# A GpSimd word read ahead of weight loads, weight-quarter sums on VectorE alone, and a re-planned order of 1,784 operations, in a chunk-selecting attention followed by a gated feed-forward layer

## The chip, the cores and the metric

The kernel runs on one core of one Trainium2 chip. The core's engines are named here as the profile names them: PE (TensorE matmuls) with PEld (its weight loads), DVE (VectorE), ACT (ScalarE), POOL (GpSimd) and SP (SyncE, which here only issues DMAs). The metric is device microseconds of one execution; the median over several executions is compared.

## The reference: what is computed

Attention over 4 batches, 8 heads, 768 positions, 64 dimensions, in which each query may only look at 6 of the 24 chunks of 32 keys, and then a gated layer over all 3072 tokens:

```python
ub = np.sum(np.maximum(q[:, :, :, None, :] * k_min[:, :, None, :, :], q[:, :, :, None, :] * k_max[:, :, None, :, :]), axis=-1)
ub = np.where(causal, ub, -1000000000.0)
top_chunks = np.argsort(ub, axis=-1)[..., -top_k:]
scores = scale * np.matmul(q, k.transpose(0, 1, 3, 2))      # only selected chunks, causal
attn = softmax(scores); attn_out = np.matmul(attn, v)
gate = 1.0 / (1.0 + np.exp(-(x @ w_gate)))                  # x: [3072, 512], w_gate: [512, 1536]
val = x @ w_val
return (gate * val @ w_out).astype(np.float32)              # w_out: [1536, 512]
```

## The kernel before, in words

**Units.** The 24 blocks of 128 queries are worked in eight units of three blocks, u0 to u7. Unit u0 (and one block of u2) holds "first" blocks, whose queries see fewer than six chunks, so that nothing is selected: function `first` turns keys and queries on PE (`kfT`, `qfT`), copies them to fp16 (`kf16`, `qf16`), makes scores (`scf`), exponentials on ACT (`expf`), zeroes the upper triangle on POOL (`cmf`), multiplies with the values (`pvf`), divides (`rzf`, `xf` on DVE), turns the result (`xpsf`) and copies it into the unit's input of the feed-forward layer (`xTf`). The other units also compute bounds for each chunk (`ub`), transpose them (`ubn`), take the eight largest (`mx`, a chain of MAX8), mark the rest (`ap`, `apt`) and add the marks to the queries (`hqm`), and then go through `attend` (scores `sc`, `exp`, triangle `cm`, values `pv`, division `rz` and `x`, turn `xps`, copy `xT`).

**Feed-forward.** For each unit, function `ffn` (lines 883 to 912) makes, for each of 12 column blocks, four matmuls `g` with the gate weights and four `v` with the value weights (line 898), a tanh on ACT (line 906) and one product on DVE (`hg`, line 910); `project_out` (lines 914 to 942) multiplies with the output weights (`o`, line 929), copies to SBUF (`osb`) and stores (`out`). Units u5 and u6 are worked together by `ffn_pair` (lines 963 to 1067) in a scheme with seven products for eight: it needs sums of quarters of the gate and value weights, four for each (`Sg0` to `Sg3`, `Sv0` to `Sv3`, function `mixed`, line 958, each 128x1536 fp16), and sums of halves of the units' inputs (`T0` to `T3`, line 980).

**Loads.** Attention inputs are loaded from SP's queue: `kf`, `qf`, `vf` for the first blocks of batches 0 to 2 (for k and q in two pieces each, 128 KB; v 256 KB), then `kq_u` for unit 1 (eight loads of 192 KB), value blocks `v`, `kq_u` for unit 2 and so on. The weights (three column parts `wg0..2`, `wv0..2` and three row parts `wo0..2`, each read as fp32 and cast to fp16, 512 KB) are loaded from POOL's queue (lines 470 to 476). A DMA issue stands in its engine's stream like any other instruction; what is behind it waits for it.

**What sets the order.** No scheduler decides at build time. A string `ORDER` (lines 94 to 258) names every operation once, in the order in which it is emitted, with `@ENGINE` where another than the first listed engine takes it and `:n` for the buffer slots. Each engine executes its own operations in that order. The dependencies that a `plan.add` lists (its `reads`, `writes` and `deps`) were for the planner that wrote the string; in the built program an instruction waits only for what it really touches: the data it reads and the buffers it overwrites. A load of weights touches nothing that an attention load writes, so in the program the weight loads wait for nothing but their place in POOL's stream, although their `plan.add` lists a load of queries (line 1087) or the operation `cmf_2_1` (line 1088) ahead of them. SP's loads reuse eight completion semaphores in turn, so each waits for the landing of the load eight places before it.

**POOL's stream at the start** of the program before: constants, the mask pattern (`epat`, line 439), two copies into the key tiles (`hkf1`, `hkp111`), `wg0`, `wv0`, the two `cmf_0`, the two `cmf_1`, `v16_0_0`, `vc_2` (the cast of the third first block's values, which waits for the load `vf_2`), the two `cmf_2`, `wg1`, `wv1`, `wg2`, `wv2`, one key copy, `wo0`, `wo1`, `wo2`.

Of the kernel before, what the change touches and what calls it, by code (L numbers as in the profile page):

```python
# [94 lines left out]
vf1_3:0 kf0_0:0 v10 ap0 vf1_2:1 ident hq1 kf1_0 epat0:0 vf1_1:2 qf0_0:1 ident16 v11 hq0 epat kcr0 qf1_0 ap1 kcr1  # L95
qf0_1:2 kf1_1:3 kfT_0:0 qf1_1 hkp001 kf0_1 hkp000 hkp101@ACT kf0_2:4 qfT_0:1 kf16_0@DVE:3 vf_1:5 hkp011 hkf0@ACT
qf16_0@DVE:4 hkf1 hkp100 hkp110@ACT scf_0:2,3,1 qf1_2:0 kxf1:0 qf0_2 expf_0_0 kxf0 hkp111@POOL kf1_2 qfT_1:4
expf_0_1:2 kcr_f vf_0:1 hkp010 kfT_1:5 qf16_1:5 wg0 wv0 kf16_1:6 vf_2:3 vc_1@ACT scf_1:6,7,3 cmf_0_0 expf_1_1:0
cmf_0_1 k1_u1:0 qfT_2:1 expf_1_0 cmf_1_1 k2_u1 kfT_2:2 cmf_1_0 qf16_2:3 pvf_1_1:0 pvf_1_0:3 kf16_2:4 rzf_1_1:0 k0_u1
v16_0_0 xf_1_1:0 scf_2:4,5,3 rzf_1_0:1 k3_u1 xf_1_0:1 xpsf_1_1:7,0 pvf_0_0:6 q2_u1 expf_2_0 xTf_1_1 pvf_0_1:1  # L100
xpsf_1_0:2 vc_2 rzf_0_0:0 q3_u1 expf_2_1:1 rzf_0_1:1 xf_0_0:2 cmf_2_0 q0_u1 xf_0_1:0 kn_u1_1:5 xpsf_0_0:0 xTf_1_0
q1_u1 xTf_0_0@ACT xpsf_0_1:3 cmf_2_1 pvf_2_0:7 kT_u1_1:4 xTf_0_1 rzf_2_0:0 wg1 xf_2_0:1 pvf_2_1:6 kt_u1_1:0 rzf_2_1:1
xpsf_2_0:5 xf_2_1:2 wv1 hk0_u1_1@ACT v_0_1:5 xTf_2_0 xpsf_2_1:1 kx1_u1_1:1 kn_u1_2:6 wg2 xTf_2_1 kn_u1_0:2 kT_u1_2:2
kx0_u1_1 wv2 hk1_u1_1@ACT g_u0_0:0,0,0 kt_u1_2:1 v_0_2:0 kn_u1_3@DVE:3 kx0_u1_2 hk1_u1_2@ACT hk0_u1_2@POOL v_u0_0:3
wo0 kx1_u1_2 tanh_u0_0 wo1 g_u0_1:7,1,1 hg_u0_0 wo2 kT_u1_0:6 tanh_u0_1 v_u0_1:5 kt_u1_0:2 g_u0_2:1,2,2 hk0_u1_0
hk1_u1_0@ACT hg_u0_1 v_u0_2:4 tanh_u0_2 kx0_u1_0 g_u0_3:2,3,3 kx1_u1_0 hg_u0_2 kT_u1_3:0 tanh_u0_3 v_u0_3:3
qn_u1_2@DVE:4 kt_u1_3:0 g_u0_4:7,0,4 hk1_u1_3 hk0_u1_3@ACT kx1_u1_3 qT_u1_2:5 tanh_u0_4 hg_u0_3 qf_u1_2:0 kx0_u1_3
v_0_3:4 qn_u1_3@POOL:5 qm_u1_2@ACT:0 hq0_u1_2@DVE hq1_u1_2 qT_u1_3:1 qn_u1_0@DVE:1 v_u0_4:6 k1_u2:1 kcr_u1 qf_u1_3
qn_u1_1@DVE:6 qT_u1_0:4 hq0_u1_3@DVE hq1_u1_3 g_u0_5:2,1,5 hg_u0_4 qf_u1_0 qm_u1_3@POOL qT_u1_1:7 tanh_u0_5 qm_u1_0
v_u0_5:3 hq0_u1_0@DVE hq1_u1_0 qf_u1_1@DVE g_u0_6:5,2,6 hg_u0_5 qm_u1_1@ACT hq0_u1_1@POOL v_u0_6:0 tanh_u0_6  # L110
hq1_u1_1@DVE ub_u1:1,6 hg_u0_6 g_u0_7:4,3,7 ubn1_u1:0 k2_u2 v16_0_1 ubn0_u1 v_u0_7:2 tanh_u0_7 k0_u2 ubm1_u1 ubm0_u1
mx1_u1:0 g_u0_8:7,0,8 mx0_u1 v_u0_8:3 tanh_u0_8 g_u0_9:5,1,9 ap1_u1 ap0_u1 hg_u0_8 v_u0_9:0 tanh_u0_9 apt0_u1:0
g_u0_10:6,2,10 apt1_u1 hg_u0_9 hqm0_u1_0@ACT hqm0_u1_2 v_u0_10:1 tanh_u0_10 hqm1_u1_0@DVE sc_u1_0_2:4,0 hqm1_u1_2@DVE
sc_u1_1_2:7,2 sc_u1_4_2:3,3 exp_u1_0_2 g_u0_11:5,0,11 hg_u0_10 exp_u1_1_2 hg_u0_7 exp_u1_4_2 sc_u1_3_2:0,1 sc_u1_3_1:6
tanh_u0_11 v_u0_11:4 exp_u1_3_2 exp_u1_3_1 k3_u2 sc_u1_0_0:1 v16_0_2 hg_u0_11 sc_u1_3_0:7 q0_u2 exp_u1_0_0 o0_u0_0:3,0
q1_u2 exp_u1_3_0 cm_u1_0 sc_u1_4_1:2 sc_u1_1_0:5 cm_u1_3 exp_u1_4_1 sc_u1_4_0:0 o1_u0_0 exp_u1_1_0 exp_u1_4_0 cm_u1_1
sc_u1_1_1:6 sc_u1_0_1:4 exp_u1_1_1 cm_u1_4 o2_u0_0 exp_u1_0_1 q2_u2 v16_0_3 o0_u0_1:1,1 v_0_4:1 osb_u0_0 kn_u2_1@DVE:2
pv_u1_3:7 out_u0_0 kn_u2_2@DVE:3 kT_u2_1:2 sc_u1_2_0:5,1 kn_u2_0@DVE:4 sc_u1_2_2:0 kt_u2_1:1 kT_u2_2:6 q3_u2
exp_u1_2_0 kT_u2_0:4 kn_u2_3@DVE:5 sc_u1_2_1:3 kx0_u2_1 hk1_u2_1@POOL o1_u0_1 v_0_5:3 exp_u1_2_2 kx0_u2_2
qn_u2_0@POOL:1 exp_u1_2_1 kx1_u2_2:0 qn_u2_1@POOL:6 kt_u2_0:2 pv_u1_1:5 kx1_u2_1 cm_u1_2 kf0_3:2 kt_u2_2:0 pv_u1_0  # L120
kx0_u2_0 hk1_u2_0@ACT kT_u2_3:0 qn_u2_2@POOL:2 kx1_u2_0 qT_u2_1:3 pv_u1_2 kx1_u2_3 hk0_u2_2@ACT hk1_u2_2@POOL kf1_3
sc_u1_5_2:2,2 qf_u2_1:1 v16_0_4 sc_u1_6_2:6,0 rz_u1_0:0 sc_u1_5_1:4 kx0_u2_3 exp_u1_5_2 o2_u0_1 qf0_3:5 kt_u2_3@DVE:0
exp_u1_5_1 hq1_u2_1@POOL x_u1_0:0 exp_u1_6_2 kcr_u2@POOL qf1_3 hk0_u2_3@POOL qT_u2_2:3 qn_u2_3:3 rz_u1_1:1
sc_u1_7_2:2,1 qm_u2_1:0 xps_u1_0:0,1 hq0_u2_1 vf_3:0 sc_u1_5_0:4 x_u1_1:1 hk0_u2_0@POOL qT_u2_3:6 xT_u1_0@ACT
sc_u1_7_0:5 qf_u2_2@DVE hk0_u2_1@POOL exp_u1_7_2 pv_u1_4:7 qf_u2_3@DVE hk1_u2_3@POOL exp_u1_5_0 xps_u1_1:0 k00_1:0
sc_u1_6_0:3 v16_0_5 osb_u0_1@DVE qT_u2_0:2 hq0_u2_3 o0_u0_2:6,0 cm_u1_5 xT_u1_1 qf_u2_0 exp_u1_7_0 qm_u2_3 qm_u2_0
pv_u1_5 qm_u2_2 hq0_u2_0 sc_u1_7_1:4 hq1_u2_3@DVE sc_u1_6_1:1 ub_u2:0,2 exp_u1_6_0 rz_u1_2:0 cm_u1_7 x_u1_2:2
exp_u1_7_1 hq0_u2_2@POOL exp_u1_6_1 hq1_u2_2@DVE pv_u1_7:5 hq1_u2_0@DVE xps_u1_2:3 out_u0_1 vc_3@ACT ubn1_u2:0 cm_u1_6
qfT_3:7 k01_1 xT_u1_2 kfT_3:4 mx1_u2:0 qf16_3:4 pv_u1_6 o1_u0_2 kf16_3:5 ubn0_u2 rz_u1_3:1 ap1_u2 x_u1_3:0 scf_3:1,2,3
o2_u0_2 apt1_u2:0 expf_3_1:2 k10_1 mx0_u2 hqm1_u2_0 expf_3_0 xps_u1_3:3 osb_u0_2 xT_u1_3 cmf_3_1 sc_u2_5_1:7,1  # L130
sc_u2_4_0:0,0 exp_u2_5_1 g_u1_0:4,1,12 ap0_u2 hqm1_u2_2@DVE exp_u2_4_0 apt0_u2 cmf_3_0 v_u1_0:5 tanh_u1_0
hqm0_u2_0@DVE g_u1_1:2,2,13 hqm0_u2_2@DVE hg_u1_0 cm_u2_4 out_u0_2 v_u1_1:1 tanh_u1_1 k11_1 sc_u2_5_2:3 pvf_3_0:6
hg_u1_1 g_u1_2:7,3,14 exp_u2_5_2 rzf_3_0:0 xf_3_0:1 v_u1_2:0 tanh_u1_2 sc_u2_0_0:4,3 hg_u1_2 sc_u2_0_1:5 q01_1:1
exp_u2_0_0 sc_u2_0_2:2 xpsf_3_0:1,0 pvf_3_1:3 g_u1_3:6,0,15 exp_u2_0_2 xTf_3_0 cm_u2_0 rzf_3_1:1 exp_u2_0_1 xf_3_1:2
v_u1_3:7 tanh_u1_3 sc_u2_1_2:0,2 sc_u2_1_0:4 hg_u1_3 exp_u2_1_2 g_u1_4:1,1,16 exp_u2_1_0 sc_u2_1_1:2 tanh_u1_4
pv_u2_0:3 cm_u2_1 xpsf_3_1:5 exp_u2_1_1 q00_1 sc_u2_4_1:6 kx0_1_1 k16_1_2:6 sc_u2_6_2:7,3 v_u1_4:0 exp_u2_4_1 kx0_1_2
k16_1_1:2 exp_u2_6_2 sc_u2_6_0:4 g_u1_5:1,2,17 xTf_3_1@ACT exp_u2_6_0 kx1_1_1:1 k16_1_3:3 v_u1_5:2 k16_1_0@ACT:1
cm_u2_6 pv_u2_1 kx1_1_2 tanh_u1_5 sc_u2_6_1:6 sc_u2_4_2:7 sc_u2_2_1:5,2 exp_u2_6_1 g_u1_6:4,3,0 kt_1_1:4 exp_u2_4_2
sc_u2_2_2:1 exp_u2_2_1 v_u1_6:6 kx0_1_0 q11_1 hk0_1_1 exp_u2_2_2 pv_u2_4:7 tanh_u1_6 sc_u2_2_0:5 kt_1_0:5 hk1_1_1
sc_u2_3_1:1,0 exp_u2_2_0 g_u1_7:4,0,1 kx1_1_0 exp_u2_3_1 hk1_1_0 sc_u2_3_2:5 tanh_u1_7 sc_u2_3_0:1 kt_1_2:0  # L140
hk0_1_0@ACT cm_u2_2 q10_1 v_u1_7:4 exp_u2_3_0 hg_u1_6 exp_u2_3_2 hk1_1_2@DVE g_u1_8:6,3,2 rz_u2_0:0 cm_u2_3 hg_u1_4
hk0_1_2@ACT sc_u2_5_0:1 x_u2_0:0 v_u1_8:5 tanh_u1_8 hg_u1_5 v_1_1:4 exp_u2_5_0 pv_u2_2:0 kt_1_3:2 xps_u2_0:3 pv_u2_3
cm_u2_5 xT_u2_0@ACT g_u1_9:6,1,3 kx0_1_3 hk1_1_3@ACT hk0_1_3 pv_u2_5 sc_u2_7_2:2,2 rz_u2_1:1 kx1_1_3 tanh_u1_9
sc_u2_7_0:1 v_u1_9:3 exp_u2_7_2 v_1_3:1 exp_u2_7_0 qf0_u3_2:0 g_u1_10:6,2,4 kcr_1@POOL k01_2:0 qf0_u4_1:1 cm_u2_7
sc_u2_7_1:2 hg_u1_9 tanh_u1_10 v16_1_1 exp_u2_7_1 qf0_u3_1 v_u1_10:1 qf0_u3_3 g_u1_11:6,1,5 qf0_u3_0 qm_u3_2@ACT:0
hq0_u3_2@POOL k00_2 x_u2_1:1 tanh_u1_11 rz_u2_2:0 hg_u1_10 hq1_u3_0@POOL pv_u2_7:3 qm_u3_0@ACT xps_u2_1:2 qf0_u4_0
v_u1_11:0 xT_u2_1 v16_1_3 hq0_u3_0@ACT x_u2_2:2 ub_u3:6,1 hg_u1_11 hq1_u3_2@POOL hg_u1_8 hg_u1_7 xps_u2_2:2 pv_u2_6
xT_u2_2 o0_u1_0:7,1 ubn0_u3:0 rz_u2_3:1 ubn1_u3 o1_u1_0 ubm0_u3 qf0_u4_3 mx0_u3:0 o2_u1_0 ubm1_u3 x_u2_3:0 o0_u1_1:0,0
mx1_u3 osb_u1_0 k10_2 ap0_u3 o1_u1_1 ap1_u3 apt0_u3:0 apt1_u3 o2_u1_1 hqm0_u3_0@DVE hqm0_u3_2@ACT hqm1_u3_2@DVE
# [1043 lines left out]
```

## Time and profile before

| | us |
|---|---|
| median of 3 runs | 299.01 (298.44 to 300.31) |
| the profiled execution, whole | 297.33 |
| its span, first to last instruction | 295.6 |
| PE busy in the span | 274.8 |
| DVE busy | 221.1 |
| ACT busy | 203.9 |
| POOL busy | 99.1 |
| granted TensorE clock | 1.0 throughout |

The profile shows one execution. Rows of its timeline give start and duration in microseconds, the engine, the source line, and the tiles written and read; a bracket gives the idle time of that engine just before and what ended it. "Landing" of a DMA is the time from its issue until its data are there. PE's spans are modelled ends, and PE instructions overlap by some 0.1 to 0.2 us in them, so the busy time of a stretch, not the sum of single durations, says how full PE is. The same holds to a smaller degree for DVE and ACT.

### The profile page before, as it was taken

What the parts mean: (1) busy time and instruction counts of PE and PEld (TensorE: products, weight loads), DVE (VectorE), ACT (ScalarE), POOL (GpSimd) and SP (SyncE); (2) the same over time, 40 slices, a digit from 0 to 9 for tenths busy, and PEclk for the clock granted to TensorE, in tenths of its full rate; (3) what the DMA queues carried; (4) which work ended last, traced back from release to release, by engine and by line L of the source; (5) the groups of instructions that cost most, each with busy time, mean ns of one, the idle gap of its engine ahead of it and who ended that gap; (6) DMA issues with size and microseconds to landing.
All of it is one profiled execution on the core that took longest, in us unless ns stands there. A gap on an engine that the chain in (4) does not pass through costs nothing.

```text
span 295.6 us, 7004 instructions
## 1 busy us (share of the span) xinstructions
PE 274.8 (93%) x2644; PEld 175.3 (59%) x2644; DVE 221.1 (75%) x620; ACT 203.9 (69%) x423; POOL 99.1 (34%) x162
## 2 busy tenths in 40 slices
...
GB/s 162 206 280 221 202 216 157 202 155 164 184 82 142 172 189 168 74 219 164 165 179 131 106 35 3 2 1 2 66 45 2 1 0 2 0 72 53 84 7 106
DMA packets 123377, 32.69 MB, mean 111 GB/s; under 512 B 111440, under 2 KB 120400, under 8 KB 123344
## 3 DMA queue, kind: packets, MB, share of 16 engines
...
q14 instruction: 13, 0.11, 0.1%
...
## 4 chain that ended last, share of the span: by engine, by line
PE 58%; DMA 15%; DVE 14%; ACT 6%; POOL 2%; issue 2%; SPq 1%; DVEq 0%; POOLq 0%; ACTq 0%
PE o_u L929 17%; PE v_u L898 9%; PE g_u L898 8%; DMA wo<-in_moe_w_out_dram 8%; PE sc_u L815 7%; PE pv_u L848 4%; DMA k<-in_k_dram 4%; DMA vf<-in_v_dram 3%; ACT att_u L826 3%; PE suv_u5u L1009 2%; PE sug_u5u L1009 2%; PE ube_u L754 2%; DVE Sg L958 2%; DVE kcr L539 1%; PE srv_u5u L1009 1%
## 5 line engine op out<-in xcount | busy, mean ns | idle before, releaser
L826 ACT ACTIVATE att_u<-sc_u 128x512 f16<-128x512 f32 (+2 forms) x184 | 88.0, 562 | 10.6 <-PE sc_u L815 10.1
L898 PE MATMUL v_u<-xT_u,wv 128*128 128x384 f16 x288 | 58.9, 327 | 2.5 <-DVE ubn_u L765 2.5
L929 PE MATMUL o_u<-wo,hg_u 128*128 128x512 f16 (+1 forms) x252 | 59.1, 376 | 1.2 <-DMA wo<-in_moe_w_out_dram 1.2
L898 PE MATMUL g_u<-xT_u,wg 128*128 128x384 f16 x288 | 59.3, 329 | 0.2 <-ACT gate_u L906 0.2
L910 DVE SCALAR_TENSOR_TENSOR hg_u<-gate_u,v_u 128x384 f16<-128x384 f16 x72 | 38.4, 539 | 27.6 <-PE v_u L898 20.2
L832 POOL TENSOR_SCALAR_AFFINE_SELECT att_u<-att_u 128x384 f16<-128x384 f16 (+1 forms) x56 | 30.0, 540 | 74.9 <-ACT att_u L826 74.1
L906 ACT ACTIVATE gate_u<-g_u 128x384 f16<-128x384 f32 x72 | 35.9, 502 | 21.2 <-PE g_u L898 16.0
L898 PEld LDWEIGHTS <-wv 128*128 128x128 f16 x288 | 27.9, 98 | 19.5 <-issue 3.6
L929 PEld LDWEIGHTS <-hg_u 128*128 128x128 f16 x264 | 24.4, 98 | 24.6 <-issue 1.4
L898 PEld LDWEIGHTS <-wg 128*128 128x128 f16 x288 | 27.6, 98 | 17.3 <-issue 1.3
L938 ACT ACTIVATE osb_u<-o_u 128x512 f32<-128x512 f32 (+1 forms) x22 | 13.2, 600 | 28.8 <-PE o_u L929 28.8
L815 PE MATMUL sc_u<-hqe,hke 128*128 128x128 f16 (+2 forms) x220 | 28.1, 243 | 0.1
L848 PEld LDWEIGHTS <-att_u 128*128 128x128 f16 x640 | 25.0, 98 | 5.2 <-ACT att_u L826 0.7
L815 PE MATMUL sc_u<-hqo,hko 128*128 128x128 f16 (+2 forms) x220 | 27.8, 243 | 0.3 <-POOL hqo L330 0.3
L848 PE MATMUL pv_u<-v,att_u 128*128 128x65 f16 x640 | 27.6, 193 | 0.1
L815 PEld LDWEIGHTS <-hke 128*128 128x128 f16 x220 | 16.5, 98 | 6.7 <-issue 0.9
L815 PEld LDWEIGHTS <-hko 128*128 128x128 f16 x220 | 16.7, 98 | 5.3 <-issue 1.0
L531 POOL CAST v<-v 128x512 f16<-128x512 f32 x23 | 14.8, 646 | 6.9 <-DMA v<-in_v_dram 6.5
L867 DVE TENSOR_TENSOR x_u<-pv_u,rz_u 128x384 f16<-128x384 f32 (+1 forms) x28 | 14.6, 523 | 0.3
L865 DVE RECIPROCAL rz_u<-pv_u 128x6 f32<-128x6 f32 (+1 forms) x28 | 5.0, 179 | 10.0 <-PE pv_u L848 9.8
L777 DVE MAX8 mx_u<-ubn_u 128x8 f32<-128x8 f32 (+16 forms) x152 | 12.4, 154 | 0.1
L539 DVE TRANSPOSE_TENSOR_REDUCE kx<-k 128x24 f32<-128x768 f32 x12 | 11.3, 952 | 0.9 <-DMA out_dram<-osb_u 0.9
...
## 6 DMA issues: line engine op xcount, KB each, us to landing
v<-in_v_dram SPq DMA_DIRECT2D x23, 256.0 KB, 5.2
out_dram<-osb_u SPq DMA_DIRECT2D x23, 256.0 KB, 2.0
...
wg<-in_moe_w_gate_dram POOLq DMA_DIRECT2D x3, 512.0 KB, 7.8
wv<-in_moe_w_val_dram POOLq DMA_DIRECT2D x3, 512.0 KB, 10.3
wo<-in_moe_w_out_dram POOLq DMA_DIRECT2D x3, 512.0 KB, 20.4
kf<-in_k_dram SPq DMA_DIRECT2D x8, 128.0 KB, 3.3
```

What stands on the lines that cost most here:

```text
L531: plan.add(f"v16_{b}_{ib}", {POOL: pool(H * D)}, lambda e: nc.gpsimd.tensor_copy(v16[b % 2][:, ib, :, 0:D], at(t)), reads=[t], writes=[("v ...
L539: plan.add(f"kx{m}_{name}_{p}", {DVE: dve(size)}, lambda e, m=m, op=op: nc.vector.tensor_reduce(out=outs[m](), in_=src(), op=op, axis=AX.X ...
L815: nc.tensor.matmul(at(t)[:, o:o + 128 * m], hk[b % 2][e_][:, p, 128 * jb:128 * jb + 128], hq[u.side][e_][:, p, 128 * x:128 * (x + m)], sta ...
L826: plan.add(f"exp_{u.name}_{h}_{y}", {ACT: act(n)}, lambda e, t=t, att=att, b0=b0, n=n: nc.scalar.activation(at(att)[:, b0:b0 + n], at(t), ...
L832: nc.gpsimd.affine_select(out=dv, in_=dv, compare_op=ALU.is_ge, fill=0.0, base=0, pattern=[[0, u.m], [1, 128]], channel_multiplier=-1)
L848: nc.tensor.matmul(at(pv)[:, last, x, :], at(att)[:, c:c + 128], v16[b % 2][:, jb, h, :], start=(jb == 0), stop=(jb == ib))
L867: plan.add(f"x_{u.name}_{p}", {DVE: dve(u.t)}, lambda e: nc.vector.tensor_tensor(at(x_).rearrange("p a (e d) -> p e a d", e=2), at(pv)[:, ...
L898: nc.tensor.matmul(at(t), w16[:, c, 128 * fb:128 * fb + 128], at(u.xt)[:, c, :], start=(c == 0), stop=(c == 3))
L906: plan.add(f"tanh_{u.name}_{fb}", {ACT: act(T)}, lambda e, g=g, gate=gate: nc.scalar.activation(at(gate), at(g), AF.Tanh, scale=0.5), read ...
L910: plan.add(f"hg_{u.name}_{fb}", {DVE: dve(T)}, lambda e, w_=w_, gate=gate, hg=hg: nc.vector.scalar_tensor_tensor(at(hg), at(gate), 1.0, at ...
L929: nc.tensor.matmul(at(o), hgs[c][1][1]()[:, 128 * tb:128 * tb + 128], wo16[:, fc, lo:hi], start=(c == 0), stop=(c == NFB - 1))
L1009: nc.tensor.matmul(at(t), left[i](c), right[i](c), start=first and c == 0, stop=c == 1, skip_group_check=not first)
```

## The change

Three edits in the code and a new `ORDER`.

**The word read.** A new operation `after` lets POOL copy one fp32 word of a loaded query tile into a small tile. `after0` reads a word of the second piece of `qf_1` and stands ahead of `wg0`; `after1` reads one of the second piece of `qf_2` and stands ahead of all later weight loads. Since POOL's stream is in order, the loads behind it then wait in fact for that landing.

**Sums on VectorE.** In `mixed` and `ffn_pair` POOL is no longer allowed for the sums. Before, seven of the eight `S` operations and the four `T` were on DVE by the order string and one, `Sv2`, on POOL; now all twelve are on DVE.

**Order.** The string is another plan of the same operations, with other slots and here and there another engine (for instance three more `xT` copies on DVE instead of ACT, five fewer 64x768 key copies on DVE).

```diff
+    word = lone("word", [1, 2], F32)
...
+    def after(i, key, prio):
+
+        plan.add(f"after{i}", {POOL: (110, 150)}, lambda e: nc.gpsimd.tensor_copy(word[0:1, i:i + 1], at(key[0])[0:1, key[1], 0:1]),
+                 reads=[key], writes=[f"after{i}"], prio=prio)
...
-            op = plan.add(f"S{name}{i}", {POOL: pool(n), DVE: dve(n, 2)}, lambda e, i=i, x=x, op=op, y=y: (
-                nc.vector if e == DVE else nc.gpsimd).tensor_tensor(at(t)[:, i], x(), y(), op),
+            op = plan.add(f"S{name}{i}", {DVE: dve(n, 1.8)}, lambda e, i=i, x=x, op=op, y=y: nc.vector.tensor_tensor(at(t)[:, i], x(), y(), op),
...
-            plan.add(f"T{i}_{tag}", {POOL: pool(2 * T), DVE: dve(2 * T, 2)}, lambda e, i=i, x=x, op=op, y=y: (
-                nc.vector if e == DVE else nc.gpsimd).tensor_tensor(at(ts)[:, i], x(), y(), op),
+            plan.add(f"T{i}_{tag}", {DVE: dve(2 * T, 2)}, lambda e, i=i, x=x, op=op, y=y: nc.vector.tensor_tensor(at(ts)[:, i], x(), y(), op),
...
-    weights(0, -0.9, [(raw_f[1]["q"], 1)])
-    last = next(op for op in plan.ops if op.name == "cmf_2_1")
+    after(0, (raw_f[1]["q"], 1), -2.0)
+    weights(0, -0.9, ["after0"])
+    after(1, (raw_f[2]["q"], 1), -0.6)
     for i in range(1, 3):
-        for op in weights(i, -0.5 + 0.2 * i, []):
-            op.deps.append((last, False))
+        weights(i, -0.5 + 0.2 * i, ["after1"])
     for i in range(3):
-        weights_out(i, 0.3, []).deps.append((last, False))
+        weights_out(i, 0.3, ["after1"])
```

The order string up to the first feed-forward matmul, new:

```diff
+vf1_3:0 kf0_0:0 ident kcr0 epat0:0 kf1_0 vf1_2:1 v10 ident16 ap1 epat qf1_0:1 ap0 qf0_0 hq1 kcr1 vf_0:2 hq0 v11 kf1_1:3
+hkp111 kf0_1 hkp110 hkp011@ACT kfT_0:0 qf1_1:4 hkp010 qf0_1 hkp000 hkp100@ACT qfT_0:1 kf16_0@DVE:2 vf1_1:3 qf16_0:4 kxf0
+hkp001@POOL hkf0@ACT kf1_2:5 kxf1:0 scf_0:2,3,1 v16_0_0 qf0_2:0 hkf1@ACT kcr_f kf0_2 hkp101 kfT_1:4 expf_0_0 qf1_2
+expf_0_1:2 after0 cmf_0_0 kf16_1@DVE:5 vf_1:1 qfT_1:5 cmf_0_1 vf_2:2 pvf_0_0:6 wg0 qf16_1:6 rzf_0_0:0 pvf_0_1:7 xf_0_0:0
+rzf_0_1:1 scf_1:1,0,3 wv0 xf_0_1:1 xpsf_0_0:2,0 expf_1_1:0 xTf_0_0 xpsf_0_1:3 expf_1_0 xTf_0_1 cmf_1_1 cmf_1_0 k1_u1:0
+k0_u1 kfT_2:4 k3_u1 after1 wg1 qfT_2:5 kf16_2:4 wv1 q0_u1 vc_1@ACT qf16_2@DVE:2 q2_u1 wg2 pvf_1_0:6 pvf_1_1:7 k2_u1
+rzf_1_0:1 scf_2:2,0,1 vc_2@ACT xf_1_0:2 wv2 q3_u1 rzf_1_1:1 expf_2_1:2 xpsf_1_0:3 xf_1_1:0 wo0 xTf_1_0 expf_2_0
+xpsf_1_1:1 xTf_1_1 cmf_2_1 cmf_2_0 pvf_2_1:4 q1_u1 kn_u1_1:5 rzf_2_1:0 wo1 pvf_2_0:5 v_0_1:3 xf_2_1:1 kn_u1_0:6
+kT_u1_1:6 rzf_2_0:1 xf_2_0:2 wo2 xpsf_2_1:7 kT_u1_0:0 kt_u1_1:0 xTf_2_1 kx0_u1_1 hk0_u1_1@ACT hk1_u1_1@POOL xpsf_2_0:3
+xTf_2_0 kt_u1_0:1 kx1_u1_1:1 g_u0_0:2,0,0 ...
```

So POOL's stream at the start is now: constants, `epat`, one key fill (`hkp001`), `v16_0_0`, `after0`, the two `cmf_0`, `wg0`, `wv0`, the two `cmf_1`, `after1`, `wg1`, `wv1`, `wg2`, `wv2`, `wo0`, the two `cmf_2`, `wo1`, `wo2`. ACT's stream up to there is: two key fills (`hkp011`, `hkp100`), `qf16_0`, `hkf0`, `hkf1`, two `expf_0`, `qf16_1`, two `expf_1`, `kf16_2`, `vc_1`, `vc_2`, two `expf_2`. SP's first fifteen loads are `kf_0` and `qf_0` (two pieces each), `vf_0`, `kf_1` and `qf_1` (two each), `kf_2` and `qf_2` (two each, mixed), `vf_1`, `vf_2`; then the eight of `kq_u` for unit 1. Before, `vf_1` stood tenth, `vf_0` fourteenth and `vf_2` fifteenth.

The eight sums stand thus in the new order: the four `Sg` around the first projection of u3, `Sv0`, `Sv1` and `Sv3` in that projection and `Sv2` between the second and third column block of u4. Before, all eight stood between the end of u3's projection and the sixth column block of u4. The attention of u7 now stands almost wholly (29 of its 32 exponentials) between `T0` and the first matmul `g_u7_0`; before, 19 stood ahead of `T0`.

327 lines of the change are left out of this document (163 added, 164 removed).

## The prediction

> **What bounds the kernel now.** I read the page's busy shares, then a table of busy time by stretches of the span, then what PE waited for, then the timeline at the two places where PE stood.
>
> ```profile
> PE 274.8 (93%) x2644; PEld 175.3 (59%) x2644; DVE 221.1 (75%) x620; ACT 203.9 (69%) x423; POOL 99.1 (34%) x162
> ```
>
> ```profile
> core 0: us, PE busy (x) PEld busy (x) DVE busy (x) ACT busy (x) POOL busy (x), PEclk, DMA share, GB/s
> 0.00:24.40 24.40, 12.62 (x89) 9.03 (x90) 15.03 (x37) 13.13 (x22) 14.67 (x29) 1.00 1.04 220
> 24.40:60.00 35.60, 33.78 (x290) 21.73 (x289) 26.91 (x86) 25.88 (x61) 15.88 (x31) 1.00 1.09 195
> 60.00:170.00 110.00, 109.09 (x1157) 70.54 (x1156) 98.08 (x288) 83.65 (x173) 47.39 (x76) 1.00 1.01 153
> 170.00:200.00 30.00, 27.50 (x354) 18.34 (x351) 29.22 (x102) 24.06 (x48) 14.65 (x17) 1.00 0.03 11
> 200.00:284.00 84.00, 83.41 (x713) 51.27 (x711) 51.26 (x111) 54.76 (x119) 6.49 (x12) 1.00 0.08 29
> 284.00:295.60 11.60, 8.39 (x52) 4.42 (x50) 0.56 (x1) 2.43 (x5) 0.00 (x0) 1.00 0.19 68
> ```
>
> ```profile
> PE pvf L618 <- POOL attf L611: 4.9, 3, 4.2
> PE v_u L898 <- DVE ubn_u L765: 2.5, 1, 2.5
> PE o_u L929 <- DMA wo<-in_moe_w_out_dram: 1.2, 1, 1.2
> ```
>
> PE is the bound: stretch length minus PE busy is 11.8 us in the first 24.4, then 1.8, 0.9, 2.5, 0.6, and 3.2 in the tail. The change adds and removes no matmul, so it can take only from these 20.8 us of idle, and can add to them. Three rows carry what is within its reach: 4.2 at the start (a wait for POOL's triangle), 2.5 in the middle (a wait for DVE's transposed bounds), 1.2 for the output weights.
>
> **The change, part by part.**
>
> *`Sv2` leaves POOL.* The middle stall:
>
> ```profile
> 178.12 3.94 POOL L958 TENSOR_TENSOR Sv<-wv 128x1536 f16<-128x1536 f16 x1
> 178.15 0.94 DVE L958 TENSOR_TENSOR Sg<-wg,Sg 128x1536 f16<-128x1536 f16 x1
> 179.49 3.39 DVE L958 TENSOR_TENSOR Sg<-wg 128x1536 f16<-128x1536 f16 x1
> 182.80 1.27 DVE L958 TENSOR_TENSOR Sv<-wv,Sv 128x1536 f16<-128x1536 f16 x1
> 184.49 0.53 DVE L765 STREAM_TRANSPOSE ubn_u<-ubo_u 128x384 f32<-128x384 f32 x1
> 184.61 0.81 PE L898 MATMUL v_u<-xT_u,wv 128*128 128x384 f16 x4 [2.50 <-DVE ubn_u L765]
> 184.95 1.00 DVE L777 MAX8 mx_u<-ubn_u 128x8 f32<-128x13 f32 x12
> ```
>
> While POOL works on `Sv2` until 182.06, a DVE sum of the same shape takes 3.39 instead of 0.94. The transposes stand behind it on DVE, and the matmul `v_u` needs the buffers that they free. In the new order no sum meets a POOL sum, the sums are spread over some 60 us, and none stands directly ahead of these transposes. DVE takes over `Sv2` (about 1.0, between 0.94 and 1.27) and gets back 3.39 - 0.94 = 2.45; cover for the 1.0 is DVE's slack in the stretch where it stands, else 1.0 is paid. I take the whole stall: -2.5 (bounds -2.5 and 0, if a wait on DVE of the same length comes elsewhere).
> [...]
>
> *Waits and weight loads at the start.* Rows in order of time (rows named SPq and POOLq are queues; a bracket is idle time):
>
> ```profile
> 0.79 0.13 POOL L593 MEMSET vf<- 128x8 f16 x1 [0.29 <-POOLq L1177]
> 4.40 1.47 ACT L326 COPY hke<-epat 64x1536 f16<-64x1536 f16 x1 [0.77 <-POOL epat L439]
> 6.18 0.62 ACT L326 COPY hke<-kf 64x512 f16<-64x512 f16 x1 [0.31 <-DVE kf L328]
> 8.08 1.06 ACT L609 ACTIVATE attf<-scf 128x512 f16<-128x512 f32 x2
> 8.55 1.00 POOL L470 DMA_DIRECT2D wg<-in_moe_w_gate_dram  x1
> 9.05 0.57 ACT L326 CAST qf<-qfT 128x512 f16<-128x512 f32 x1
> 10.22 5.77 SPq L505 DMA_DIRECT2D kq_u<-in_k_dram  x4
> 16.03 4.34 SPq L505 DMA_DIRECT2D kq_u<-in_q_dram  x4
> 20.04 0.62 POOL L330 CAST vf<-vf 128x512 f16<-128x512 f32 x1 [5.50 <-DMA vf<-in_v_dram]
> 20.61 1.23 POOL L611 TENSOR_SCALAR_AFFINE_SELECT attf<-attf 128x512 f16<-128x512 f16 x2
> 21.78 0.77 POOL L470 DMA_DIRECT2D wg<-in_moe_w_gate_dram  x1
> 24.61 0.85 PE L898 MATMUL g_u<-xT_u,wg 128*128 128x384 f16 x2
> ```
>
> ```profile
> 9.80 10.19 DMA vf<-in_v_dram
> ```
>
> ```profile
> wv<-in_moe_w_val_dram POOLq DMA_DIRECT2D x3, 512.0 KB, 10.3
> wo<-in_moe_w_out_dram POOLq DMA_DIRECT2D x3, 512.0 KB, 20.4
> vf<-in_v_dram SPq DMA_DIRECT2D x4, 256.0 KB, 4.8
> qf<-in_q_dram SPq DMA_DIRECT2D x8, 128.0 KB, 3.2
> ```
>
> The load `vf_2`, issued at 9.80 behind `wg0` (8.55), takes 10.19 against a median of 4.8; POOL stands 5.50 for it, and the triangle, the last matmuls `pvf` and everything up to `g_u0_0` at 24.61 follow. In the changed order:
> 1. ACT. `epat` is done about 0.35 earlier (two small fills now stand behind it), at 4.0. Then two fills at 1.47, `qf16_0` 0.57, two key copies at 0.62, both `expf_0` in 1.06: 4.0 + 2.94 + 0.57 + 1.24 + 1.06 = 9.8, against 9.14 before. With a little issue time I use 9.9.
> 2. POOL. `after0` waits for a piece of `qf_1`, issued by about 4.5 and 3.2 on its way: 7.7, ahead of the triangle's 9.9. The read itself is a tiny copy; the nearest row is the fill of 8 elements, 0.13. So I cost both reads at 0 (bounds 0 and 2 x 0.13; cover: POOL's waits for ACT). What delays `wg0` is its place behind `cmf_0`: triangle done at 10.6, issues at 10.6 and about 11.6, two us later than before. `wv0` lands by its row at 11.6 + 10.3 = 21.9, still ahead of its use at about 22.7.
> 3. `expf_1` ends near 12.9, `cmf_1` 13.5, `after1` 13.6 (its piece of `qf_2` landed long ago). Five issues at 0.77 until 17.4 are queued ahead of `cmf_2`, on which PE waits: 17.4 + 1.23 = 18.6.
> 4. From the triangle's end to `g_u0_0` it was 24.61 - 21.84 = 2.77; so `g_u0_0` starts at 21.4, 3.2 earlier.
> This needs `vf_2` early. It is issued near 8.5, ahead of both weight loads; its cast now stands on ACT ahead of `expf_2`. At 4.8 it lands at 13.3, unnoticed. At 10.19 it lands at 18.7, and cast, exponential and triangle then bring `g_u0_0` to where it was. I take -2.8, near the full gain, since the weights that shared the queues with it now start two us behind it; bounds -3.2 and 0.
>
> *Later weights.* The landing of `wo2` cost PE 1.2. Its issue moves from about 27 to 19, but the transfers stand in a row in a nearly full DMA (share 1.04 and 1.09), so I take half: -0.6 (bounds -1.2 and 0).
>
> *The rest of the order.* No row shows it. For the gain the nearest rows are the idle of 24.4 to 170 and 200 to 284 outside the wait for `wo`: 0.9 + 0.6 = 1.5 at most can vanish. For a loss it is DVE (rivals). More work is packed on DVE early, so I take +1.0 rather than zero.
>
> Sum: -2.8 - 2.5 - 0.6 + 0 + 1.0 = -4.9 against the profiled execution's 297.33 gives 292.4. That execution lies 1.68 below the median of the runs; on the median's scale, 299.01 - 4.9 = **294.1 us**.
>
> **Rivals.**
> *DVE becomes the bound (ends on the other side).* From the first output projection of u1 to `g_u3_0`, I counted the new order's operations and multiplied by rows:
>
> ```profile
> L910 DVE SCALAR_TENSOR_TENSOR hg_u<-gate_u,v_u 128x384 f16<-128x384 f16 x72 | 38.4, 539 | 27.6 <-PE v_u L898 20.2 <-ACT osb_u L938 5.9 <-ACT gate_u L906 1.2
> L539 DVE TRANSPOSE_TENSOR_REDUCE kx<-k 128x24 f32<-128x768 f32 x12 | 11.3, 952 | 0.9 <-DMA out_dram<-osb_u 0.9
> L705 DVE STREAM_TRANSPOSE kt<-k 128x768 f16<-128x768 f16 x12 | 11.4, 947 | 0.0
> ```
>
> 14 products at 0.54, 8 reductions and 4 key transposes at 0.95, 6 MAX8 chains at 1.00, 12 transposes at 0.53 to 0.57, and 60 smaller ones of 0.18 to 0.68 (23.5 together): 55.2 us, over 51.1 of PE at the spacing that four such matmuls have in a row. If each is paid singly (a MAX8 chain 1.6, being issued apart) it is 58.8. The order before had 71.6 over 67.1 in its densest stretch and stood 2.5 there, so a ratio of 1.07 to 1.08 alone need not stop PE: DVE may run late and catch up. If it does stop it: +4.1, 298.2. If single durations must be paid, +7.7, and +0.5 where the next stretch has 61.1 over 60.6: 302.3. It decides against the change once DVE costs PE 4.9, and by over 1% from 7.9. Chance 0.24: 0.13 at 298.2, 0.11 at 302.3.
>
> *The queries of unit 1 arrive late.* SP's eight loads start about 1.2 earlier, but the weights now run beside them from 10.6 without the gap of 10 to 22.
>
> ```profile
> kq_u<-in_q_dram SPq DMA_DIRECT2D x4, 192.0 KB, 6.8
> kq_u<-in_q_dram SPq DMA_DIRECT2D x4, 128.0 KB, 15.2
> ```
>
> At 6.8 (unit 1 before) the last lands near 26; at the 15.2 that unit 2's loads took beside the weights, at 34.4, with 192 KB in proportion to 128 at 42. Their copies are due near 31.4, so 3.0 to 10.6 late; I take 5.2, nearer the first: 299.3. Chance 0.15. Against it: SP's queue is served beside POOL's from the start.
>
> *Issues held by DVE.* [...] The row at 8.55 shows 1.00 instead of 0.77, no more. [...] The trace has one mild case among nine, so 0.06.
>
> *It doesn't do what it says.* Neither read ever waits, `vf_2` is late all the same, and the stall in the middle only moves: 299.0, chance 0.02.
>
> **How the numbers follow.** Forecast 0.53, at 294.1; its own range is 290.6 (299.01 - 3.2 - 2.5 - 1.2 - 1.5) to 296.0. A measurement tells about 1% from no change, so faster is below 296.0, slower above 302.0. Faster 0.53; same 0.13 + 0.15 + 0.02 = 0.30; slower 0.11 + 0.06 = 0.17. The range of 8 in 10 reaches from 290.6 to 301.0, over the two middle cases; what lies above is 0.17.
>
> **What would show it.** In the changed profile: `g_u0_0` near 21.8 rather than 24.6; `wg` issues at 10.6 and 11.6 and five more at 0.77 without a wait between; `vf_2` landed by 15; no sum above 1.3; no PE wait for `ubn_u` of 2.5; the wait for `wo` under 1.2. Wrong would be: PE waits for DVE between u1's and u3's projection that add to over 4, waits for `kq_u` copies before 40, `wg` issues above 1.3, or a late triangle `cmf_2`.

## The result and the profile after

| | before | after |
|---|---|---|
| median of the paired runs, us | 299.65 (298.44 to 300.31, 4 runs) | 296.39 (295.60 to 297.38, 4 runs) |
| ratio, 95% interval | | 0.9897 (0.9849 to 0.9946) |
| the profiled execution, us | 297.33 | 296.52 |
| its span, us | 295.6 | 294.7 |
| first feed-forward matmul `g_u0_0` starts at, us | 24.61 | 22.61 |

The change makes the kernel about 1% faster, 3.3 us; the forecast was 4.9, at 294.1. That forecast was counted from a before of 299.01; from there the measured ratio leads to 295.9. A second set of paired runs (`after_again`) gave a ratio of 0.9888 (0.9846 to 0.9930).

The DMA line in slices of before, then the busy shares, the clock and the DMA line of the profile after:

```profile
DMA  7999998999939899499898400000110000011202
```

```profile
PE 274.2 (93%) x2644; PEld 174.4 (59%) x2644; DVE 219.2 (74%) x617; ACT 207.5 (70%) x425; POOL 94.9 (32%) x165
...
PEclk9977999999999999999999999999999999999999
DMA  7999999999999999909999510000110000011202
```

The same stretches as in the prediction, after (length, then busy time of each engine, granted clock, DMA share, GB/s):

```profile
0.00:24.40 24.40, 13.88 (x96) 9.74 (x97) 17.63 (x43) 14.61 (x23) 17.07 (x33) 0.87 1.08 214
24.40:60.00 35.60, 34.51 (x339) 22.64 (x338) 26.40 (x91) 26.59 (x65) 14.22 (x30) 0.99 1.16 207
60.00:170.00 110.00, 105.19 (x1079) 67.08 (x1078) 97.94 (x280) 86.39 (x173) 46.39 (x76) 1.00 1.15 148
170.00:200.00 30.00, 29.16 (x379) 19.28 (x378) 27.31 (x100) 22.06 (x43) 9.68 (x13) 1.00 0.05 20
200.00:284.00 84.00, 84.00 (x714) 51.78 (x712) 49.59 (x109) 55.87 (x121) 7.51 (x14) 1.00 0.08 29
284.00:294.70 10.70, 7.48 (x47) 3.94 (x45) 0.34 (x1) 1.96 (x4) 0.00 (x0) 1.00 0.20 74
```

What PE waited for, after (total, times, longest):

```profile
PE xps_u L880 <- DVE x_u L872: 2.4, 3, 1.4
PE pvf L623 <- POOL attf L616: 2.3, 3, 1.9
...
PE pv_u L853 <- POOL att_u L837: 1.3, 2, 1.0
...
PE o_u L934 <- DMA wo<-in_moe_w_out_dram: 0.7, 1, 0.7
```

Length minus PE busy, before and after: 11.78 and 10.52 up to 24.4; 1.82 and 1.09 to 60; 0.91 and 4.81 to 170; 2.50 and 0.84 to 200; 0.59 and 0.00 to 284; 3.21 and 3.22 in the tail. The forecast's two stalls have shrunk, and 3.9 us of new idle time stand between 60 and 170, all of it before 120. In the row of DMA the two hollows of before (a slice of 3 tenths at 81 us, one of 4 at 118) are gone: the DMA engines now work without a pause until about 126 us, and the one hollow up to 160 lies behind that.

The differences sum to -0.34 us, PE's own busy time is 0.56 less, together the 0.9 by which the spans differ. That is less than the 3.3 of the medians: the profiled execution of before, 297.33, was 1.3 to 2.3 us faster than the medians of its runs (298.67 to 299.65 in four sets of runs), that after was not. Stretches and marks below compare single executions; times compare medians.

### The profile page after: what moved, and what is told of

It reads as the page before. It is cut to its first block, busy times and chain, and to the rows that moved or that the text cites. A ratio compares the mean times of both kernels' runs of the same rounds, so it can differ in the third digit from the quotient of the medians.

```text
span 294.7 us, 7019 instructions
## 1 busy us (share of the span) xinstructions
PE 274.2 (93%) x2644; PEld 174.4 (59%) x2644; DVE 219.2 (74%) x617; ACT 207.5 (70%) x425; POOL 94.9 (32%) x165
## 4 chain that ended last, share of the span: by engine, by line
PE 60%; DMA 15%; DVE 7%; SPq 6%; ACT 5%; POOL 4%; issue 2%; POOLq 0%; DVEq 0%; ACTq 0%
PE o_u L934 16%; DMA wo<-in_moe_w_out_dram 9%; PE g_u L903 9%; PE v_u L903 9%; PE sc_u L820 8%; SPq L520 6%; PE pv_u L853 5%; DMA k<-in_k_dram 3%; PE sug_u5u L1012 3%; PE suv_u5u L1012 3%; DMA v<-in_v_dram 2%; ACT att_u L831 2%; PE ube_u L759 2%; PE xps_u L880 1%; DMA q<-in_q_dram 1%
## 5 line engine op out<-in xcount | busy, mean ns | idle before, releaser
L831 ACT ACTIVATE att_u<-sc_u 128x512 f16<-128x512 f32 (+3 forms) x184 | 89.9, 549 | 15.1 <-PE sc_u L820 14.6
L837 POOL TENSOR_SCALAR_AFFINE_SELECT att_u<-att_u 128x384 f16<-128x384 f16 (+1 forms) x56 | 29.2, 529 | 100.4 <-ACT att_u L831 98.2
L934 PE MATMUL o_u<-wo,hg_u 128*128 128x512 f16 (+1 forms) x252 | 59.8, 376 | 1.0 <-DMA wo<-in_moe_w_out_dram 0.7
L820 PE MATMUL sc_u<-hqo,hko 128*128 128x128 f16 (+2 forms) x220 | 28.6, 243 | 0.9 <-ACT att_u L831 0.8
L820 PE MATMUL sc_u<-hqe,hke 128*128 128x128 f16 (+2 forms) x220 | 26.4, 243 | 0.0
L726 DVE STREAM_TRANSPOSE qf_u<-q 128x384 f32<-128x384 f32 (+2 forms) x28 | 10.9, 430 | 2.9 <-issue 2.1
## 6 DMA issues: line engine op xcount, KB each, us to landing
wo<-in_moe_w_out_dram POOLq DMA_DIRECT2D x3, 512.0 KB, 24.4
```

Of the source, the lines that this page charges most:

```text
L820: nc.tensor.matmul(at(t)[:, o:o + 128 * m], hk[b % 2][e_][:, p, 128 * jb:128 * jb + 128], hq[u.side][e_][:, p, 128 * x:128 * (x + m)], sta ...
L831: plan.add(f"exp_{u.name}_{h}_{y}", {ACT: act(n)}, lambda e, t=t, att=att, b0=b0, n=n: nc.scalar.activation(at(att)[:, b0:b0 + n], at(t), ...
L837: nc.gpsimd.affine_select(out=dv, in_=dv, compare_op=ALU.is_ge, fill=0.0, base=0, pattern=[[0, u.m], [1, 128]], channel_multiplier=-1)
L934: nc.tensor.matmul(at(o), hgs[c][1][1]()[:, 128 * tb:128 * tb + 128], wo16[:, fc, lo:hi], start=(c == 0), stop=(c == NFB - 1))
```

## The experiments

Each ratio is to the kernel before, run in turn with it on the same chip. Three groups ran on three chips; a difference between two kernels counts only where their intervals stand apart.

| kernel | median, us | before, us | ratio, 95% interval |
|---|---|---|---|
| b_sv2_dve | 296.65 | 299.03 | 0.9907 (0.9874 to 0.9939) |
| h_start_pool | 296.26 | 299.03 | 0.9915 (0.9885 to 0.9945) |
| h_start_dve | 295.90 | 299.03 | 0.9898 (0.9862 to 0.9935) |
| a_noread | 296.50 | 299.03 | 0.9904 (0.9867 to 0.9941) |
| h_k1 | 294.79 | 298.69 | 0.9877 (0.9835 to 0.9918) |
| a_k1 | 296.46 | 298.69 | 0.9947 (0.9915 to 0.9979) |
| a_k1q2 | 303.47 | 298.69 | 1.0164 (1.0106 to 1.0222) |
| a_warm | 295.48 | 298.69 | 0.9887 (0.9854 to 0.9920) |
| a_k1_q1 | 296.07 | 298.67 | 0.9886 (0.9840 to 0.9932) |
| h_k1_warm | 296.07 | 298.67 | 0.9892 (0.9846 to 0.9939) |
| a_sv2_pool | 296.43 | 298.67 | 0.9914 (0.9883 to 0.9944) |
| after_again | 295.30 | 298.67 | 0.9888 (0.9846 to 0.9930) |

### The middle stall: b_sv2_dve

```diff
-... Sv2 ...
+... Sv2@DVE ...
```

> The kernel before with one edit: Sv2 on VectorE instead of GpSimd, at the same place in the order. Theory (the contention makes the middle stall): the sum Sg2 falls from 3.39 to about 0.95, PE's wait of 2.50 for ubn_u goes, DVE takes about 1.0 more in the same stretch; 1.5 to 2.5 us faster than before, ratio 0.992 to 0.995. Rival (the eight sums stand too densely, whichever engine takes them): the transposes still come late and a wait for ubn_u of over 1.5 stays; less than 1 us faster.

The row of the stretch with the stall, in b_sv2_dve:

```profile
170.00:200.00 30.00, 29.92 (x387) 20.16 (x385) 29.16 (x106) 26.41 (x53) 11.89 (x17) 1.00 0.03 11
```

Idle time fell from 2.50 to 0.08. The copies of the output blocks show that nothing else moved: the last of u3 starts at 171.4 in both, the first of u4 at 203.3 instead of 205.7, the last of u7 at 290.1 instead of 292.4. One word in the order is worth 2.4 us, in the profile and in the medians. (All six runs of b_sv2_dve had a recorded clock of 0.998 or more; against the runs of before with such a clock, median 298.53, it is 1.9.) The first theory holds, and the forecast's 2.5 was near.

### The start alone: h_start_pool and h_start_dve

The new order up to `g_u0_0`, then the order of before; two buffers get another slot. Two operations that the order of before has ahead of `g_u0_0`, `kn_u1_2` and `kT_u1_2`, stay ahead of it.

```diff
-vf1_3:0 kf0_0:0 v10 ap0 ... hk1_u1_1@ACT g_u0_0:0,0,0 ... kt_u1_2:1 ... Sv2
+vf1_3:0 kf0_0:0 ident kcr0 ... kn_u1_2:6 kT_u1_2:2 g_u0_0:1,0,0 ... kt_u1_2:2 ... Sv2@POOL
```

> The new order only up to the first feed-forward matmul, with both word reads; from there the order of before, Sv2 on GpSimd. Theory (the start's gain is kept to the end): the first g_u near 22.6 and the time 2.0 to 2.6 us below before, ratio about 0.992. Rival (the gain at the start is handed back where the loads of keys and queries come late, between 60 and 120 us): g_u as early, the time less than 1 us below before, with new PE idle between 60 and 120.

> As h_start_pool, and Sv2 on VectorE. If both gains are real, lie one behind the other and nothing gives them back: their sum, 4 to 5 us below before, ratio about 0.985, which would be faster than the whole change (0.9897). If the loads hand the start's gain back: only the middle's 1.5 to 2.5, ratio 0.992 to 0.995.

h_start_dve won 3.1 us, no more than the whole change and not the 4 to 5 that its expectation gives for both gains. Three things were not as expected. `g_u0_0` came at 23.95 in h_start_pool and 23.77 in h_start_dve, not near 22.6, because the key turn `kT_u1_2` stands ahead of it. With `Sv2` still on GpSimd the stall was nearly gone (idle 0.95 between 170 and 200), so the 2.8 us of h_start_pool, though near the first theory's 2.0 to 2.6, are not the start's gain alone. The sums in h_start_pool:

```profile
179.11 4.80 POOL L963 TENSOR_TENSOR Sv<-wv 128x1536 f16<-128x1536 f16 x1
179.14 0.94 DVE L963 TENSOR_TENSOR Sg<-wg 128x1536 f16<-128x1536 f16 x1
180.01 0.94 DVE L963 TENSOR_TENSOR Sv<-wv,Sv 128x1536 f16<-128x1536 f16 x1
```

Here POOL's sum is the one that stretches, 4.80, and DVE's two keep their 0.94. Last, the start's gain is handed back, with the order of before unchanged from `g_u0_0` on. Last copy of u0, first reduction of k of batch 1 on DVE, first copy of u1, in before:

```profile
65.95 0.60 ACT L938 ACTIVATE osb_u<-o_u 128x512 f32<-128x512 f32 x1
73.95 1.84 DVE L539 TRANSPOSE_TENSOR_REDUCE kcr<-k 128x24 f32<-128x768 f32 x2
95.23 0.60 ACT L938 ACTIVATE osb_u<-o_u 128x512 f32<-128x512 f32 x1 [3.68 <-PE o_u L929]
```

and in h_start_dve:

```profile
64.25 0.60 ACT L944 ACTIVATE osb_u<-o_u 128x512 f32<-128x512 f32 x1
73.33 1.84 DVE L545 TRANSPOSE_TENSOR_REDUCE kcr<-k 128x24 f32<-128x768 f32 x2 [1.14 <-DMA k<-in_k_dram]
94.72 0.60 ACT L944 ACTIVATE osb_u<-o_u 128x512 f32<-128x512 f32 x1 [3.68 <-PE o_u L935]
```

1.7 us ahead at 64, 0.6 at the reduction, which stood 1.14 for its load, 0.5 at the first output of u1. The rival of the expectation holds: the gain goes where k comes late.

### Sv2 back on GpSimd in the new order: a_sv2_pool

```diff
-            op = plan.add(f"S{name}{i}", {DVE: dve(n, 1.8)}, lambda e, i=i, x=x, op=op, y=y: nc.vector.tensor_tensor(at(t)[:, i], x(), y(), op),
+            op = plan.add(f"S{name}{i}", {DVE: dve(n, 1.8)}, lambda e, i=i, x=x, op=op, y=y: (nc.vector if e == DVE else nc.gpsimd).tensor_tensor(at(t)[:, i], x(), y(), op),
...
-... Sv2 ...
+... Sv2@POOL ...
```

> The changed kernel with Sv2 alone back on GpSimd, at its place of the new order. In h_start_pool, with Sv2 on GpSimd and the other sums beside it as before, the stall had shrunk to under 1 us: the sum of DVE that was issued 0.03 after Sv2 was not held, that on GpSimd took 4.80. Theory (whoever comes first holds the other, so the cost is an accident of timing): an operation of DVE with two inputs in SBUF stretches to 2 to 3 us and up to 1.5 us are lost, or GpSimd's sum stretches and nothing is lost. Forecast's reading (always held, a stall of 2.5): 2 to 2.5 us slower than the changed kernel.

Timeline of a_sv2_pool:

```profile
180.05 3.09 POOL L962 TENSOR_TENSOR Sv<-wv 128x1536 f16<-128x1536 f16 x1
180.30 3.15 DVE L787 TENSOR_TENSOR ap<-ubn_u,mx_u 128x288 f16<-128x288 f32 x1
```

The comparison `ap`, 0.45 when alone, was issued 0.25 behind POOL's sum and ended 0.31 after it (183.45 against 183.14). PE's idle time from 170 to 200 rose to 2.24, from 0.85 in after_again, and the median was 1.1 us above after_again on the same chip; the intervals overlap. `Sg2` in before shows the same, 182.88 against 182.06. A DVE sum issued only 0.03 behind POOL's went first (h_start_pool, and in before the sum at 178.15). So in these runs what a POOL sum cost went by which of the two began first: DVE's operation kept its time when issued 0.03 behind, and stretched when issued 0.25 behind. The theory of the expectation holds; the stretched operation, 3.15, lies a little above its 2 to 3, and the loss near its upper end.

### The word reads: a_noread

```diff
-    after(0, (raw_f[1]["q"], 1), -2.0)
-    after(1, (raw_f[2]["q"], 1), -0.6)
```

> The changed kernel without the two word reads; the order of all other operations is the same, so the weight loads then wait for nothing but their place on GpSimd. Forecast (place, not wait): the same within 0.5 us of the changed kernel, wg0 again issued near 11.8 behind the triangle. Rival (the reads hold the weights off): wg and wv issue over 1 us earlier, the loads beside them come later, and the time moves by over 1 us.

The triangle ahead of `wg0`, and `wg0`, in a_noread:

```profile
10.76 1.22 POOL L616 TENSOR_SCALAR_AFFINE_SELECT attf<-attf 128x512 f16<-128x512 f16 x2 [3.10 <-ACT attf L614]
11.93 0.92 POOL L475 DMA_DIRECT2D wg<-in_moe_w_gate_dram  x1
```

With the reads, in the changed kernel:

```profile
8.48 0.18 POOL L470 COPY word<-qf 1x1 f32<-1x1 f32 x1 [0.88 <-DMA qf<-in_q_dram]
10.70 1.22 POOL L616 TENSOR_SCALAR_AFFINE_SELECT attf<-attf 128x512 f16<-128x512 f16 x2 [2.04 <-ACT attf L614]
11.87 0.93 POOL L475 DMA_DIRECT2D wg<-in_moe_w_gate_dram  x1
...
15.05 0.76 POOL L475 DMA_DIRECT2D wg<-in_moe_w_gate_dram  x1
...
18.75 1.27 POOL L616 TENSOR_SCALAR_AFFINE_SELECT attf<-attf 128x512 f16<-128x512 f16 x2
19.49 0.40 PE L623 MATMUL pvf<-vf,attf 128*128 128x65 f16 x4 [1.91 <-POOL attf L616]
...
22.61 1.44 PE L903 MATMUL g_u<-xT_u,wg 128*128 128x384 f16 x4 [0.38 <-DVE xT_u L327]
```

Without its read POOL waits 3.10 for ACT instead of 0.88 and 2.04. The weights start at the same time: the place in the stream holds them, not the wait, as forecast. In the profiled run of a_noread `v_u0_0` then waited 1.90 for `wv0`, in the changed kernel 0.40, although both issued it at 12.8; the medians agree within 0.1, and one profiled run can't tell whether this has to do with the reads.

### The late loads: h_k1, a_k1, a_k1q2, a_k1_q1

What DVE waited for between 60 and 125, in before and then in the changed kernel:

```profile
DVE hg_u L910 <- PE v_u L898: 6.5, 3, 5.3
```

```profile
DVE kx L544 <- DMA k<-in_k_dram: 3.2, 2, 2.4
DVE qf_u L726 <- issue: 2.1, 1, 2.1
...
DVE qf_u L726 <- DMA q<-in_q_dram: 0.8, 1, 0.8
```

Before, DVE mostly waited for PE there; after, it waited 4.0 for loads and 2.1 for something that the profile does not name. PE itself waited for no load: in the list of PE's waits after, 1.8 us of `xps_u` and the 1.3 of `pv_u` fall here, and the operations of DVE and POOL that it waited for stood in their streams behind work on k and q. h_k1 and a_k1 move three loads ahead of two stores in SP's queue, in h_start_dve and in the changed kernel:

```diff
-... k00_1 out_u0_1 k01_1 k10_1 out_u0_2 k11_1 q00_1 ...
+... k00_1 k01_1 k10_1 k11_1 out_u0_1 out_u0_2 q00_1 ...
```

> h_start_dve, with three of the four loads of k for batch 1 moved in SyncE's queue to directly behind the first, so ahead of the stores of u0's second and third block, each of which waits there for its output. In h_start_dve u0's output was 1.7 us earlier than before and the first reduction of k only 0.6, with DVE idle 1.1 for the load. Theory Q (the queue's order makes the load late): DVE's wait for k goes, u1's first output comes about 1 us earlier, the time falls by about 1 us, to near 294.9. Theory B (the DMA engines are full from the start, so the load lands when its bytes are through): k lands less than 0.5 us earlier, the wait stays, the time is within 0.5 us of 295.9.

> The changed kernel with the same move of the loads of k. There DVE stood 2.4 us for k at 72 us and PE idled 2.6 us between 70 and 90. Theory Q: that wait goes and 1 to 2.5 us with it, ratio to before 0.982 to 0.987. Theory B: k lands less than 0.5 us earlier, within 0.7 us of the changed kernel. Third theory (VectorE's work itself is the bound there): the wait goes, PE's idle time between 70 and 90 stays.

h_k1:

```profile
63.65 0.60 ACT L944 ACTIVATE osb_u<-o_u 128x512 f32<-128x512 f32 x1
71.60 1.84 DVE L545 TRANSPOSE_TENSOR_REDUCE kcr<-k 128x24 f32<-128x768 f32 x2
...
85.43 0.91 DVE L727 STREAM_TRANSPOSE qf_u<-q 128x384 f32<-128x384 f32 x2 [0.89 <-DMA q<-in_q_dram]
...
93.89 0.60 ACT L944 ACTIVATE osb_u<-o_u 128x512 f32<-128x512 f32 x1 [3.69 <-PE o_u L935]
```

The wait for k is gone, as theory Q has it. Of 2.3 us ahead of before at 64, 1.3 are left at 94; in h_start_dve it was 0.5 of 1.7. So the loss on this stretch is 1.0 instead of 1.2. The rest of h_k1's lead over h_start_dve stood already at u0's first output copy (49.19 against 49.79), before the moved loads were issued (from 54.4 on). The median, 294.79, is the best of this study and near theory Q's 294.9, but the move explains only some 0.2 us of it by 94, and the intervals of h_k1 and h_start_dve overlap. The next load, q of batch 1, now makes DVE wait 0.9.

In a_k1 the wait went as well, and nothing was won. DVE's next load, and PE's longest wait in the same place:

```profile
85.02 2.15 DVE L726 STREAM_TRANSPOSE qf_u<-q 128x384 f32<-128x384 f32 x5 [3.52 <-DMA q<-in_q_dram]
```

```profile
PE g_u L903 <- DVE hg_u L915: 2.2, 1, 2.2
```

The stall has only moved on to q. PE was busy for 1.78 of the 4 us from 84 to 88, and then its granted clock fell (third column from the right), which in the changed kernel it does not here:

```profile
88.00:92.00 4.00, 3.49 (x19) 1.24 (x23) 4.00 (x12) 3.94 (x6) 2.61 (x5) 0.64 1.49 142
```

The four loads of q of batch 1 in SP's queue, in the changed kernel and in a_k1:

```profile
65.31 13.44 SPq L520 DMA_DIRECT2D q<-in_q_dram  x4
```

```profile
68.16 9.51 SPq L520 DMA_DIRECT2D q<-in_q_dram  x4
```

They begin 2.9 us apart and are all issued at 78.75 and 77.67, almost together, although one such issue can take as little as 0.43 (the fourth of k in the changed kernel). The DMA share was 1.02 to 1.63 in every 4 us from 60 to 84 in both. My reading is that each theory of the expectation was right in one half: the queue's order sets when k lands, and what the DMA engines still have to move sets when k and q together are there. The second half is read from these rows; no run changed the amount of data.

a_k1_q1 then puts q's transposes behind other work on DVE, and with them three operations of ACT and POOL that use one of them; here in the order of DVE's operations:

```diff
-qf0_u3_1 qf0_u4_1 qf0_u3_3 qf0_u4_0 qf0_u3_2 hg_u1_7 kt_1_3 hg_u1_4 ... qf0_u4_3
+hg_u1_7 kt_1_3 hg_u1_4 qf0_u3_1 qf0_u3_3 qf0_u3_2 ... qf0_u4_3 qf0_u4_1 qf0_u4_0 qf0_u4_2
```

> a_k1, and on VectorE the transposes of q for batch 1 moved behind three products and a key transpose of u1 (those for u4 further behind). In a_k1 DVE stood 3.5 us for that load at 85 us, and PE 2.2 us for a product queued behind it. Theory (the new order asks on DVE for a load that the DMA engines can't have brought by then, and holds other work behind it): PE's wait for hg goes, 1 to 2.2 us less than the 296.5 of a_k1. Rival (PE has no other work there, the queries bound the stretch): the wait comes back at the bounds ub or the scores behind them; within 0.5 us of a_k1.

a_k1_q1:

```profile
85.53 1.50 DVE L726 STREAM_TRANSPOSE qf_u<-q 128x384 f32<-128x384 f32 x3 [2.35 <-DMA q<-in_q_dram]
87.06 0.74 ACT L558 ACTIVATE qm_u<-qf_u 128x640 f32<-128x640 f32 x1 [3.17 <-DVE qf_u L726]
89.92 1.87 PE L934 MATMUL o_u<-wo,hg_u 128*128 128x512 f16 x4 [3.30 <-ACT gate_u L911]
```

Now ACT stands for q, and a tanh `gate` that is queued behind it holds PE 3.30. PE's idle time from 84 to 92 is 3.30, against 2.73 in a_k1. The median is 0.4 below a_k1's and the ratio lower by 0.006, but the intervals overlap. The rival holds in the main, though the wait came back at an output projection and not at `ub` or the scores: DVE's wait for q ends between 84.2 and 85.5 in the changed kernel, a_k1, a_k1_q1 and h_k1, and some engine with work queued behind it waits.

a_k1q2 moves the loads of q for batch 2 as well:

```diff
-... k11_2 out_u1_0 q00_2 out_u1_1 q01_2 q10_2 out_u1_2 q11_2 ...
+... k11_2 q00_2 q01_2 q10_2 q11_2 out_u1_0 out_u1_1 out_u1_2 ...
```

> a_k1, and the four loads of q for batch 2 moved ahead of the three stores of u1. In the changed kernel they landed at 113.3 and PE stood 1.38 for what is queued behind them on DVE. Theory Q: also that stall goes, 0.7 to 1.4 us less than a_k1. Theory B: the landing moves by less than 1 us, no change.

SP's queue in a_k1q2, and PE's longest wait between 60 and 125:

```profile
95.03 12.66 SPq L520 DMA_DIRECT2D q<-in_q_dram  x4
```

```profile
PE v_u L903 <- ACT osb_u L943: 5.1, 1, 5.1
```

No theory had this. Four loads took 12.66 us to issue; the stores stood behind them, so the two output buffers stayed full, ACT stood 6.1 at the next copy for a store to land, and PE 5.1 behind that: 7 us slower than a_k1 on the same chip.

### The clock at the start: a_warm, h_k1_warm

The granted clock in stretches of 2 us, in the changed kernel (last three columns: clock, DMA share, GB/s):

```profile
16.00:18.00 2.00, 1.05 (x17) 0.47 (x13) 1.61 (x6) 1.62 (x5) 2.00 (x3) 1.00 1.19 225
18.00:20.00 2.00, 0.40 (x4) 0.24 (x4) 0.07 (x1) 0.47 (x2) 2.00 (x5) 0.57 1.18 231
20.00:22.00 2.00, 1.93 (x14) 1.81 (x15) 1.66 (x6) 0.77 (x2) 1.65 (x4) 0.50 1.19 231
```

PE was busy for 1.05 of 2 us and then for 0.40, the clock read 0.57 and then 0.50, and the first two feed-forward groups took 1.44 us instead of the 0.81 of the next ones. Eight of ten runs of the changed kernel had a mean recorded clock of 0.983 to 0.988.

Groups of that length also stand where the record shows no dip. In the profile of before it reads 1.00 throughout, yet the first group took nearly twice 0.81 there too:

```profile
24.61 1.49 PE L898 MATMUL g_u<-xT_u,wg 128*128 128x384 f16 x4
```

b_sv2_dve, h_start_pool (1.49) and a_noread (1.44 to 1.49 for its first five groups) are like it, all at a recorded 1.00. So runs can't be sorted by their recorded mean with any safety. Before's 33 runs at 0.999 or 1.0 had a median of 298.31 and its 23 at 0.994 one of 299.74; but the six runs of a_sv2_pool at 1.0 and its six below had 296.26 and 296.43, and in a_noread the three at 1.0 were the slower ones (297.29 against 295.41).

```diff
+        for i in range(24):
+            nc.tensor.matmul(at(warm)[:, 128 * (i % 4):128 * (i % 4) + 128], ident16, ident16, start=True, stop=True)
...
-... cmf_2_0 pvf_2_1:4 ...
+... cmf_2_0 warm:4 pvf_2_1:4 ...
```

> The changed kernel with 24 extra matmuls of 128x128x128 on TensorE ahead of the last pair of pvf at the start, where it stood 1.91 us; their result is not used. Theory (the granted clock of 0.50 between 18 and 25 us comes from a thinly used TensorE there): the clock stays 1.0 in all runs and about 1 us is won. Rival (the clock has other causes): clocks of 0.98 to 0.99 over the span go on in most runs, and the time is the same or up to 1 us longer.

> h_k1 with the 24 extra matmuls of a_warm. If the clock at the start is what they mend, and its gain is not handed back now that k comes early: 0.5 to 1 us below the 294.8 of h_k1, near 294, ratio to before 0.983 to 0.987, clocks near 1.0. Otherwise the same as h_k1.

In a_warm:

```profile
17.05 1.50 PE L1095 MATMUL warm<-ident 128*128 128x128 f16 x24
...
22.09 0.81 PE L904 MATMUL g_u<-xT_u,wg 128*128 128x384 f16 x4 [0.70 <-DVE xT_u L328]
23.98 0.82 PE L904 MATMUL v_u<-xT_u,wv 128*128 128x384 f16 x4 [1.08 <-DMA wv<-in_moe_w_val_dram]
```

In the profiles of a_warm and h_k1_warm the first group takes 0.81; in all the twelve others it takes 1.31 or more. So the pace is kept with the filler matmuls and lost without them; that thin use of PE just ahead (1.05 and 0.40 us busy of 2) is what costs it is my reading of these runs. The recorded clock of a_warm was 0.988 or more in all 12 runs, but 0.999 or 1.0 only in seven, not in all as the theory had it. The time did not follow: 0.9887 against 0.9897 and 0.9888 for the changed kernel. The row of `v_u` shows one reason in the profiled run: the faster PE met `wv0`, not yet landed. h_k1_warm did not confirm its expectation either: its profiled run, at clock 1.0, was the fastest of all (293.46), its median 296.07. In before, an idle time of PE of 4.24 us ends at 21.30, 3.3 us ahead of the group of 1.49. In the changed kernel no single idle time was that long: the longest of PE after 10 us is 1.91.

### The changed kernel once more: after_again

> The changed kernel itself, unaltered, beside the others on one chip: near 296.4, ratio to before 0.990, clock under 1.0 in most runs.

Its ratio repeats the first within 0.001; the median is 1.1 below the expectation's.

## Why the prediction was right or wrong

**Right within its range.** 296.39 lies in 290.6 to 301.0, 2.3 above the forecast, and beyond the upper end of the likeliest case's own range (296.0) by 0.4. That is in part luck: the range is 10 us wide and reaches from clearly faster to no change, and one term of the sum was off by about 3 us.

*Start, forecast -2.8: a gain of 2.0 at* `g_u0_0`. The mechanism was as told: `vf_2` was there before its cast at 15.06, POOL issued five weight loads at 0.75 to 0.78, then the triangle. It came 1.2 later than worked out, since the scores of the first block stood 2.2 us for the key cast on DVE and so `wg0` was issued at 11.87 instead of 10.6. What failed is that a gain at `g_u0_0` was carried to the end unpriced. In the changed kernel u0's last output copy came 3.6 us ahead of before (62.39 against 65.95) and u1's first only 0.7 (94.49 against 95.23); in h_start_dve 1.2 of 1.7 us were gone by then.

*Middle, forecast -2.5:* 2.4 when done alone; idle time fell by 1.66 in the new order. All four pairs seen (two in before) fit an operation that stood until the other was through: by that reading the 3.39 of `Sg2` holds the time that it stood, and it ended 0.82 behind POOL's sum. What I had not seen is that the stall was an accident of the order of arrival, which a shift of 1 us (h_start_pool) undid by itself. The one word `Sv2@DVE` alone has a ratio of 0.9907, which the intervals do not tell apart from that of the whole change.

*Later weights, forecast -0.6:* the wait fell from 1.18 to 0.70. *Word reads, forecast 0:* right; one took 0.18, both hidden.

*The rest of the order, forecast +1.0:* this is the term that was mis-sized. Idle time between 60 and 120 rose by 3.9. I looked for the loss in DVE's work and counted it; DVE was no fuller there than before (51.0 of 60 us, before 51.1) but stood 4 us for k and q, and 2.1 more ahead of the transposes of q for batch 2. I had noted that the DMA engines were nearly full up to 170, with a share of 1.01 to 1.09, and used this only for the weights. As I read it now, it bounds the loads of batch 1 and 2 too, and an order that reaches them earlier finds them not there.

*The profiled run's offset, +1.68:* added without thought to the changed kernel. The offset belongs to one execution of before; how much of it is the clock no run shows (before's runs at a recorded 0.999 or 1.0 had a median of 298.31, those at 0.994 one of 299.74).

*Rivals.* DVE as the bound of u1 to u3: half right, place and sign, wrong cause. Late queries of unit 1: no wait for them is among PE's. Issues held by DVE, in the sum for slower with 0.06: no run shows such a hold; the weight issues of the changed kernel up to the triangle took 0.75 to 0.93 each.

What stays open: how much of the run-to-run spread of 3 to 4 us is the clock; whether it is the amount of data or the queue that makes q late; what the 2.1 ahead of q for batch 2 waited for; and whether h_k1, with the best median, beats the changed kernel; their intervals overlap.
